# A four-batch attention and two mixture layers on one core: batch 0's queries and keys kept on chip, its v sums on VectorE, whole-word byte operations, and a new order for the ramp

## The chip, the core and the metric

One core of a Trainium2 chip runs the whole program. Its engines work from queues of their own, each strictly in order: TensorE (PE, with its weight loads as PEld), VectorE (DVE), ScalarE (ACT), GpSimd (POOL), and SyncE (SP), which here only starts transfers. POOL's queue can start transfers too, among them those that add what they bring to what already stands in SBUF. The metric is the device time of one execution in microseconds, and the median of several executions counts.

## The reference, cut to what matters

```python
# q, k, v: [4 batches, 8 heads, 576 rows, 64]
q_d, k_d, v_d = mean of q, k, v over groups of 4 rows          # 144 rows
out_d  = softmax(q_d @ k_d.T / 8) @ v_d                        # full attention, down-sampled
out_up = repeat(out_d, 4 times)
out_local = softmax(q @ k.T / 8, where |i - j| < 4) @ v        # a band of 7
x = (out_up + out_local) as [2304 tokens, 512]
# first layer, d_ff 2048
h = x @ w_in;  g = s * relu(h)**2 + b;  y = g @ w_out
# second layer, d_ff 1536
out = ((y @ w_a) * (y @ w_b)) @ w_out2
```

The weights arrive as 64-bit floats and are brought to a 32-bit format on chip. Each 32-bit matmul is made of three, from a high and a low part of either operand.

## The kernel before, in words

**Stages.** The first 768 tokens (the ramp: eight tiles of 96 rows, six of batch 0 and two of batch 1) get their attention at the start, while the weights of the first layer come in. `down(b, hp, ...)` is the down-sampled attention of one head pair `hp` of batch `b`, `tile_job` the local attention of a 96-row tile on TensorE. The later rows get their local attention on VectorE (`unit`), spread over the first layer's run. That layer works through six blocks of 384 tokens; in each, 16 iterations (`a_iter`) make a slice `h` of d_ff by 12 matmuls (L1030 to L1032), the square on ScalarE (L1047 to L1054), its low part `gl` on VectorE (L1058), and 12 matmuls that add to `acc` (L1073 to L1075). The second layer follows, from about 541 us on.

**Weights.** The first layer has 32 slices, two for an iteration (one of w_in, one of w_out). `w_words` unpacks the 64-bit words of a slice of 512 KB: `z_fn` (ScalarE, L334) scales the high word, `a_fn` (ScalarE, L345, called the byte operation here) turns some of the low bits of the high word into a number in the low word, `s_fn` (VectorE, L350) makes the sign, `b_fn` (VectorE, L358) puts the parts together. Then `h_fn` (ScalarE, L374) and `l_fn` (VectorE, L379) make the high and the low part. The finished slices stay in slots of the tag `w`, of which there are 33, for all six blocks, so this is done once. Before the change `a_fn` has four forms, by `k % 4`: it reads 16-bit halves or single bytes, and writes whole 32-bit words or 16-bit halves.

**The ramp.** For a head pair of batch 0, k and q are loaded (L271) into `dk` and `dq` and summed over groups of four rows on VectorE (L572, into `kd`, `qd`). v of a head pair comes in two loads `dv` and is summed by two additions on GpSimd (L595, L596, into `vp`). The scores go through TensorE (L610), the maximum (VectorE L624, L627), the exponentials (ScalarE L637), the normalisation (VectorE L645 to L652), transposes (TensorE L661, ScalarE L673), the product with `vp` (TensorE L681, `o`), and a copy into `up` (ScalarE L693). For each of the eight tiles q and k come again, as `tq` and `tk` (192 and 204 KB); scores at L760 over a mask (L754), maximum at L773, exponentials at L787, normalisation at L795 to L802, transposes at L810 and L820, product with `tv` at L828, and the sum with `up` at L842, which gives `x`; L493 and L497 split it. For batch 1 and later the sum of v over groups of four is made by transfers (`pool_in`): SP brings the first row of each group into `pv` (L539), and six transfers from POOL's queue (L541) add the three others, two chains of three.

**What sets the order.** No order is written out. Every piece of work is a task with an engine, an estimated duration, buffers that it takes and frees, and a due time. `Program.order` plans them all by a greedy rule: it takes the task that can start first, by due time among equals, and gives out the instructions in that order; each engine's queue is the result. Due times come from `target(idx)`, the planned time of an iteration, `T0` plus a number of `STEP`s, less the constants `DUE_*`; a planned result can be used `SEEN` later. The tables give the buffers of each tag, `MAX_STAGED` how many raw slices may be in SBUF. Before the change the planner has the adding transfers on an engine of their own, `GQ`, though they stand in POOL's queue.

## Time and profile before

| | |
|---|---|
| median of three runs | 978.01 us (977.96 to 978.42) |
| the profiled execution | 977.19 us |
| its span | 975.4 us |
| mean granted TensorE clock | 0.977 of full speed |
| busy: PE, DVE, ACT, POOL | 95%, 81%, 53%, 8% of the span |
| last weight slice of the first layer finished | 170.6 us from the span's start |
| first iteration of blocks 0 to 5 begins | 84.7, 171.3, 253.0, 327.9, 405.6, 474.1 us |
| the first layer's last iteration ends, about | 541 us |

Times in the trace are counted from the start of the span; the profiled execution takes 1.8 us more than its span, and stands 0.8 us below the median. In the views a group of instructions is named by line, engine and operation, with the tile it writes, an arrow, and the tiles it reads; what follows in brackets is the idle time of the engine just before it, and the work that ended that idle time. The granted clock is a share of 2.4 GHz. PE's busy time at half the clock counts double what the same work takes at the full one.

### The profile page before, as it was taken

To read this page: it belongs to the slowest core of one execution; us is meant where nothing else is said; L and a number is where in the kernel's file an instruction comes from. 1 tells how busy PE (TensorE), PEld (TensorE's weight loads), DVE (VectorE), ACT (ScalarE), POOL (GpSimd) and SP (SyncE) were. 2 spreads that over 40 slices of the span, in tenths; PEclk is the share of its full clock that TensorE was granted. 3 is DMA by queue.
4 is the path that set the end of the run, shared out by engine and by line. 5 is a ranking of instruction groups with operands and counts; after the bars stand their busy time and mean duration, and the time that the engine had idled before them with its cause. 6 is when DMAs were issued, how large, how long until landed. Compare 5 with 4: busy or idle time off the path is not lost.

```text
span 975.4 us, 14509 instructions
## 1 busy us (share of the span) xinstructions
PE 930.3 (95%) x5371; PEld 858.5 (88%) x5371; DVE 787.2 (81%) x1377; ACT 520.4 (53%) x1144; POOL 76.7 (8%) x86
## 2 busy tenths in 40 slices
PE   8589699999899999999999999999999999999997
PEld 4357699999799999999999999998999998999995
DVE  5378888899999999997776899978977779777753
...
GB/s 181 151 231 201 275 165 44 199 78 89 147 106 100 121 121 66 98 65 51 164 169 230 229 72 124 64 22 23 173 22 23 22 22 11 98 22 23 0 1 66
DMA packets 48159, 99.19 MB, mean 102 GB/s; under 512 B 6536, under 2 KB 22248, under 8 KB 47704
## 3 DMA queue, kind: packets, MB, share of 16 engines
...
q8 instruction: 42, 0.69, 0.3%
...
## 4 chain that ended last, share of the span: by engine, by line
PE 79%; DVE 9%; ACT 5%; DMA 3%; issue 2%; POOL 1%; SPq 0%; ACTq 0%; POOLq 0%
PE ab L1304 26%; PE h L1030 6%; PE h L1032 6%; PE acc L1073 6%; PE h L1031 6%; PE acc L1074 6%; PE acc L1075 6%; PE acc L1446 5%; PE acc L1445 5%; PE acc L1444 5%; DMA pv<-in_vd_dram 2%; ACT w L345 1%; DVE pr L940 1%; DVE xo L1181 1%; PE sc L610 1%
## 5 line engine op out<-in xcount | busy, mean ns | idle before, releaser
L1304 PE MATMUL ab<-xo,w 128*128 128x384 f32 x1370 | 276.9, 339 | 1.0 <-DVE w L1334 0.5
L1304 PEld LDWEIGHTS ab<-xo,w 128*128 128x128 f32 x1370 | 246.7, 189 | 16.9 <-DVE u L1378 0.8
L1030 PE MATMUL h<-xsh,w 128*128 128x384 f32 x384 | 132.8, 346 | 1.6 <-ACT u L1047 0.8
L1073 PE MATMUL acc<-gh,w 128*128 128x384 f32 (+1 forms) x384 | 132.5, 345 | 0.5 <-ACT w L345 0.5
L1074 PE MATMUL acc<-gl,w 128*128 128x384 f32 x384 | 130.3, 339 | 0.7 <-DVE gl L1058 0.7
L1032 PE MATMUL h<-xsh,w 128*128 128x384 f32 x384 | 130.4, 340 | 0.2 <-DVE w L379 0.2
L1031 PE MATMUL h<-xsl,w 128*128 128x384 f32 x384 | 130.4, 340 | 0.0
L1075 PE MATMUL acc<-gh,w 128*128 128x384 f32 (+1 forms) x384 | 129.9, 338 | 0.0
L1047 ACT ACTIVATE u<-h 128x384 f32<-128x384 f32 x96 | 48.1, 501 | 123.2 <-PE h L1032 118.3
L1420 ACT ACTIVATE gh<-u 128x384 fp32r<-128x384 f32 x68 | 35.8, 526 | 90.5 <-DVE u L1381 54.4
L1030 PEld LDWEIGHTS h<-xsh,w 128*128 128x128 f32 x384 | 73.3, 191 | 4.8 <-issue 2.3
L1073 PEld LDWEIGHTS acc<-gh,w 128*128 128x128 f32 x384 | 72.5, 189 | 2.6 <-issue 1.3
L1074 PEld LDWEIGHTS acc<-gl,w 128*128 128x128 f32 x384 | 72.6, 189 | 1.6 <-DVE gl L1058 1.6
L1032 PEld LDWEIGHTS h<-xsh,w 128*128 128x128 f32 x384 | 73.2, 191 | 0.6 <-DVE w L379 0.6
L1031 PEld LDWEIGHTS h<-xsl,w 128*128 128x128 f32 x384 | 73.3, 191 | 0.0
L1075 PEld LDWEIGHTS acc<-gh,w 128*128 128x128 f32 x384 | 72.5, 189 | 0.0
L1058 DVE TENSOR_TENSOR gl<-u,gh 128x384 fp32r<-128x384 f32 x96 | 54.0, 562 | 16.8 <-ACT gh L1054 16.5
L1328 ACT ACTIVATE w<-ab 128x384 f32<-128x384 f32 x32 | 15.7, 491 | 92.9 <-PE ab L1304 89.0
L345 ACT ACTIVATE w<-w 128x512 int32<-128x512 uint8 (+3 forms) x63 | 63.6, 1025 | 0.0
L350 DVE TENSOR_SCALAR w<-w 128x512 uint16<-128x512 f32 x63 | 47.5, 765 | 14.2 <-ACT w L345 14.0
L1054 ACT ACTIVATE gh<-u 128x384 fp32r<-128x384 f32 x96 | 50.6, 528 | 2.4 <-PE acc L1075 0.4
L1051 ACT ACTIVATE u<-u 128x384 f32<-128x384 f32 x96 | 50.7, 528 | 1.9
...
## 6 DMA issues: line engine op xcount, KB each, us to landing
...
```

The costliest lines, as they stand in the source:

```text
L345: A_.activation(out=halves()[:, :, 0] if k % 2 else low, in_=src, func=ACTF.Copy, scale=scale, bias=bias)
L1030: nc.tensor.matmul(out=st["h"], lhsT=w[:, 0, k], rhs=hi[:, k], start=(k == 0), stop=False)
L1031: nc.tensor.matmul(out=st["h"], lhsT=w[:, 0, k], rhs=lo[:, k], start=False, stop=False)
L1032: nc.tensor.matmul(out=st["h"], lhsT=w[:, 1, k], rhs=hi[:, k], start=False, stop=(k == HP - 1))
L1051: A_.activation(out=st["u"], in_=st["u"], func=ACTF.Square)
L1054: A_.activation(out=st["hi"][:, :n], in_=st["u"], func=ACTF.Copy)
L1058: V.tensor_tensor(out=st["lo"], in0=st["u"], in1=st["hi"][:, :n].bitcast(F32), op=ALU.subtract)
L1073: nc.tensor.matmul(out=acc, lhsT=wh, rhs=st["hi"], start=(f == 0), stop=False)
L1074: nc.tensor.matmul(out=acc[:, :n], lhsT=wh, rhs=st["lo"], start=False, stop=False)
L1075: nc.tensor.matmul(out=acc, lhsT=wl, rhs=st["hi"], start=False, stop=(f == FA - 1))
L1304: nc.tensor.matmul(out=o, lhsT=w[:, k], rhs=x, start=(not more and k + n == 0), stop=(k == 1 and n == 2), skip_group_check=more,)
L1444: nc.tensor.matmul(out=acc, lhsT=gh, rhs=w[:, 0], start=first, stop=False)
```

## The change

1. **q and k of batch 0 stay.** The loads of `down(0, hp, ...)` go into eight of the `w` slots (`wide_in`), with nothing to wait for, and stay there until all six tiles of batch 0 have their scores (`free_fn` then frees the slots). These tiles have no `tq` and `tk` loads any more; their score matmuls read a window of the kept k and q, 99 or 102 columns wide.
2. **v of batch 0 is summed on VectorE**, by one `tensor_reduce` of 72x512 into 72x128 for each of the eight halves, in place of two additions on GpSimd.
3. **The byte operation** has one form: it reads 16-bit halves and writes whole 32-bit words. Its planned duration goes from 0.9 to 0.56 us.
4. **The adding transfers** are planned on POOL, 1.25 us each, with a result that counts as landed 6.0 us later; `GQ` is gone.
5. **The ramp is planned anew**: `T0`, `STEP`, `LEAD`, the due times, `MAX_STAGED` (3 to 4), the buffers of `dq`, `dk`, `tq`, `tk`. Batch 1's down-sampled attention is due relative to `target(FA)`, the start of block 1, and no longer to `target(0)`, the start of block 0.

```diff
 DOWN_ENG = [("DVE", "DVE")] * 4
-MAX_STAGED = 3
+MAX_STAGED = 4
-T0, STEP = 36.0, 3.95 / 384
-LEAD = 20.0
-DUE_DOWN = (12.0, 2.5, 0.0, 8.0)
-DUE_TILE = (4.0, 5.0, 25.0)
-DUE_JOB = (14.0, 12.0, 15.0)
+T0, STEP = 40.2, 4.018 / 384
+LEAD = 26.6
+DUE_DOWN = (12.1, 7.8, 2.1, 22.5)
+DUE_NEXT = (60.0, 0.0)
+DUE_TILE = (8.3, 20.6, 22.0)
+DUE_JOB = (11.6, 11.7, 14.9)
...
         def a_fn(picks):
             low = st["low"] = words()[:, :, 0]
-            if k % 4 < 2:
-                src, scale, bias = halves()[:, :, 1], 2.0 ** -13, -4095.5 * 2.0 ** -13
-            else:
-                src = st["s"].rearrange("p a m -> p (a m)").bitcast(U8).rearrange("p (m c) -> p m c", c=8)[:, :, 3]
-                scale, bias = 2.0 ** -5, -15.5 * 2.0 ** -5
-            A_.activation(out=halves()[:, :, 0] if k % 2 else low, in_=src, func=ACTF.Copy, scale=scale, bias=bias)
-
-        add("ACT", 0.9, a_fn, [("st", k)], [("low", k)])
+
+            A_.activation(out=low, in_=halves()[:, :, 1], func=ACTF.Copy, scale=2.0 ** -13, bias=-4095.5 * 2.0 ** -13)
+
+        add("ACT", 0.56, a_fn, [("st", k)], [("low", k)])
...
+    def wide_in(p):
+        return slot(p[0], F32).rearrange("p a m -> p (a m)")[:, :S]
...
                 t[kh] = add(
-                    "GQ" if r else "SP", 1.3, fn, (), [("pv", b)] if r == 3 else (), () if r + kh else [("pv",)], (), due,
-                    [t[kh]] if r else [t[0]] if kh else after,
+                    "POOL" if r else "SP", 1.25, fn, (), [("pv", b)] if r == 3 else (), () if r + kh else [("pv",)], (), due,
+                    [t[kh]] if r else [t[0]] if kh else after, seen=6.0,
                 )
...
-            st["k"] = new(ph, "dk", [128, S])
+            st["k"] = whole["k", b, hp] = wide_in(p) if b == 0 else new(ph, "dk", [128, S])
...
-        load(l_q, 128 * HP * TQ * 4, writes=[("tq", i)], acq=[(names["tq"],)], after=after)
-        load(l_k, 128 * HP * TW * 4, writes=[("tk", i)], acq=[(names["tk"],)], after=after)
+        if b:
+            load(l_q, 128 * HP * TQ * 4, writes=[("tq", i)], acq=[(names["tq"],)], after=after)
+            load(l_k, 128 * HP * TW * 4, writes=[("tk", i)], acq=[(names["tk"],)], after=after)
+
+        k0, k1 = max(0, 3 - t0), min(TW, S + 3 - t0)
...
-                        out=sc[h][:, hp], lhsT=st["q"][h * D:h * D + D, hp], rhs=st["k"][h * D:h * D + D, hp],
+                        out=sc[h][:, hp, k0:k1], lhsT=qk("q", hp)[h * D:h * D + D], rhs=qk("k", hp)[h * D:h * D + D],
...
     for hp in range(HP):
-        down(0, hp, "r", DOWN_ENG[hp], "POOL", target(0) - DUE_DOWN[0] + DUE_DOWN[1] * hp)
+        down(0, hp, "r", DOWN_ENG[hp], "DVE", target(0) - DUE_DOWN[0] + DUE_DOWN[1] * hp)
...
-    pool_in(1, P.made["open", "r"], target(0))
+    pool_in(1, P.made["open", "r"], target(FA) - DUE_NEXT[0])
     for hp in range(HP):
-        down(1, hp, "r", ("POOL", "POOL"), "POOL", target(0))
+        down(1, hp, "r", ("POOL", "POOL"), "POOL", target(FA) - DUE_NEXT[0] + DUE_NEXT[1] * hp)
```

How the order of the queues changes shows at three places. On SP, the first transfers of the program; `dk`, `dq`, `tq`, `tk` are batch 0's k and q before. Before:

```order
L271 DMA dk<-in_kT_dram 128x576
L271 DMA dq<-in_qT_dram 128x576
L292 DMA tq<-in_bmask_dram 96x306
L271 DMA tq<-in_tq_dram 128x384
L271 DMA tk<-in_tk_dram 128x408
L271 DMA dk<-in_kT_dram 128x576
L271 DMA dq<-in_qT_dram 128x576
L271 DMA tq<-in_tq_dram 128x384
L271 DMA tk<-in_tk_dram 128x408
L287 DMA ident<-in_ident_dram 128x128
```

and after, where `w` is one of the kept slots:

```order
L272 DMA w<-in_kT_dram 128x576
L272 DMA w<-in_qT_dram 128x576
L272 DMA w<-in_kT_dram 128x576
L272 DMA w<-in_qT_dram 128x576
L272 DMA w<-in_kT_dram 128x576
L272 DMA w<-in_qT_dram 128x576
L272 DMA w<-in_kT_dram 128x576
L272 DMA w<-in_qT_dram 128x576
L293 DMA tq<-in_bmask_dram 96x306
L288 DMA ident<-in_ident_dram 128x128
```

All k and q of batch 0 now go out first; the mask and the identity matrix follow them. On POOL, from its first work on; `dv` and `vp` are batch 0's v sums, `pv` the adding transfers for batch 1. Before:

```order
L595 TENSOR_TENSOR dv<-dv 72x256
L596 TENSOR_TENSOR vp<-dv 72x128
L595 TENSOR_TENSOR dv<-dv 72x256
L596 TENSOR_TENSOR vp<-dv 72x128
L541 DMA pv<-in_vd_dram 72x4x128
L595 TENSOR_TENSOR dv<-dv 72x256
L596 TENSOR_TENSOR vp<-dv 72x128
L541 DMA pv<-in_vd_dram 72x4x128
L595 TENSOR_TENSOR dv<-dv 72x256
L596 TENSOR_TENSOR vp<-dv 72x128
L541 DMA pv<-in_vd_dram 72x4x128
```

and after, where L577 and L578 are batch 1's sums of k and q:

```order
L544 DMA pv<-in_vd_dram 72x4x128
L577 ISA
L577 TENSOR_TENSOR dk<-dk 128x144x2
L578 TENSOR_TENSOR kd<-dk 128x144
L577 TENSOR_TENSOR dq<-dq 128x144x2
L578 TENSOR_TENSOR qd<-dq 128x144
L544 DMA pv<-in_vd_dram 72x4x128 x4
L577 TENSOR_TENSOR dk<-dk 128x144x2
L578 TENSOR_TENSOR kd<-dk 128x144
L577 TENSOR_TENSOR dq<-dq 128x144x2
L578 TENSOR_TENSOR qd<-dq 128x144
L544 DMA pv<-in_vd_dram 72x4x128
```

Nothing of batch 0 stands in POOL's queue any more. On PE, around the first matmuls `h` of block 0; `o<-w,pv` belongs to batch 1's down-sampled attention, `pw` is a filler that reads zeros. Before:

```order
L760 MATMUL sc<-tk,tq 96x102 x8
L266 LDWEIGHTS wz
L266 MATMUL pw<-wz 128x408
L681 MATMUL o<-w,pv 64x144 x4
L1030 MATMUL h<-xsh,w 128x384
L1031 MATMUL h<-xsl,w 128x384
```

and after, where `o<-w,tv` is the product of a tile of batch 0:

```order
L850 MATMUL o<-w,tv 64x96 x8
L1052 MATMUL h<-xsh,w 128x384
L1053 MATMUL h<-xsl,w 128x384
L1054 MATMUL h<-xsh,w 128x384
L1052 MATMUL h<-xsh,w 128x384
L1053 MATMUL h<-xsl,w 128x384
L1054 MATMUL h<-xsh,w 128x384
L613 MATMUL sc<-kd,qd 72x144 x4
L664 MATMUL at<-ident,w 72x72 x8
L684 MATMUL o<-w,pv 64x144 x4
```

Before, all of batch 1's outputs stand ahead of the first `h`; after, half an iteration's `h` comes first, and batch 1's outputs lie among block 0's iterations.

## Rows read from the trace of the kernel before

**Rows 1.** Busy time by stretch: us, then PE, PEld, DVE, ACT, POOL; clock; DMA.

```profile
core 0: us, PE busy (x) PEld busy (x) DVE busy (x) ACT busy (x) POOL busy (x), PEclk, DMA share, GB/s
0.00:13.17 13.17, 8.97 (x43) 4.35 (x45) 4.30 (x11) 0.00 (x0) 0.20 (x4) 0.98 0.59 187
13.17:60.00 46.83, 32.29 (x273) 20.30 (x275) 23.08 (x54) 24.59 (x117) 22.15 (x30) 0.82 0.64 162
60.00:85.00 25.00, 24.15 (x247) 15.73 (x244) 23.15 (x54) 24.28 (x82) 6.67 (x8) 1.00 0.87 284
85.00:120.00 35.00, 26.02 (x170) 23.72 (x168) 28.46 (x58) 34.97 (x99) 4.87 (x3) 0.85 0.68 212
120.00:171.00 51.00, 50.40 (x309) 48.96 (x310) 42.35 (x79) 49.25 (x91) 3.59 (x3) 1.00 0.39 114
171.00:253.00 82.00, 76.88 (x457) 74.05 (x456) 77.07 (x106) 37.01 (x85) 13.51 (x13) 0.99 0.45 137
253.00:328.00 75.00, 74.85 (x438) 71.42 (x437) 69.49 (x92) 32.14 (x78) 15.19 (x14) 0.94 0.37 92
328.00:406.00 78.00, 78.00 (x496) 73.77 (x495) 75.89 (x134) 38.89 (x106) 10.57 (x11) 1.00 0.35 105
406.00:541.00 135.00, 134.96 (x775) 134.24 (x774) 103.80 (x152) 91.60 (x165) 0.00 (x0) 1.00 0.42 144
541.00:975.00 434.00, 423.76 (x2183) 391.99 (x2182) 339.61 (x647) 187.65 (x331) 0.00 (x0) 0.99 0.15 53
```

**Rows 2.** Last unpacking step of the last weight slice, timeline of DVE.

```profile
169.90 0.69 DVE L379 TENSOR_TENSOR w<-z,w 128x512 fp32r<-128x512 f32 x1 [0.15 <-ACT w L374]
```

**Rows 3.** ACT's first work, timeline of ACT, and the wait behind it, of DVE.

```profile
11.41 0.21 DVE L288 CAST identb<-ident 96x96 bf16<-96x96 f32 x1 [1.94 <-DMA ident<-in_ident_dram]
...
13.17 1.28 ACT L637 ACT_TABLE_LOAD   x1 [13.17 <-DVE nb L627]
```

**Rows 4.** ACT's waits, 13.2 to 60: total us, times, longest.

```profile
ACT up L693 <- PE o L681: 11.5, 3, 7.8
ACT w L820 <- DVE tnb L773: 3.6, 1, 3.6
```

**Rows 5.** PE's longest waits of that stretch, timeline of PE.

```profile
40.57 0.75 PE L681 MATMUL o<-w,vp 72*64 72x144 f32 x4 [7.68 <-POOL vp L596]
...
53.06 0.47 PE L681 MATMUL o<-e,vp 72*64 72x144 f32 x4 [4.06 <-POOL vp L596]
```

**Rows 6.** POOL between 28 and 41, its timeline; then the adding transfers' landing.

```profile
28.23 1.22 POOL L541 DMA_DIRECT2D pv<-in_vd_dram  x1 [4.80 <-DMA pv<-in_vd_dram]
...
38.02 1.21 POOL L541 DMA_DIRECT2D pv<-in_vd_dram  x1 [3.32 <-issue]
38.80 1.19 POOL L595 TENSOR_TENSOR dv<-dv 72x256 f32<-72x256 f32 x1
40.07 0.45 POOL L596 TENSOR_TENSOR vp<-dv 72x128 f32<-72x128 f32 x1
...
pv<-in_vd_dram POOLq DMA_DIRECT2D x6, 144.0 KB, 5.3
```

**Rows 7.** The byte operation to 170.5 by form: count, busy us, mean ns.

```profile
L345 ACT ACTIVATE w<-w 128x512 uint16<-128x512 uint8 x8 | 11.0, 1377 | 0.0
L345 ACT ACTIVATE w<-w 128x512 uint16<-128x512 uint16 x8 | 11.0, 1375 | 0.0
...
L345 ACT ACTIVATE w<-w 128x512 int32<-128x512 uint16 x8 | 5.7, 709 | 0.0
L345 ACT ACTIVATE w<-w 128x512 int32<-128x512 uint8 x8 | 5.7, 708 | 0.0
```

**Rows 8.** Two groups of DVE to 170.7, with idle time before them.

```profile
L773 DVE TENSOR_REDUCE tnb<-sc 96x4 f32<-96x408 f32 x16 | 8.5, 567 | 12.2 <-PE sc L760 12.2
...
L572 DVE TENSOR_REDUCE kd<-dk 128x144 f32<-128x576 f32 x4 | 3.0, 738 | 2.2 <-DMA dk<-in_kT_dram 2.2
```

**Rows 9.** Timeline of PE: block 0's first matmul, and two long waits.

```profile
84.68 0.44 PE L1030 MATMUL h<-xsh,w 128*128 128x384 f32 x1
...
104.75 1.92 PE L828 MATMUL o<-w,tv 102*64 102x96 f32 x16 [6.81 <-ACT w L820]
...
252.12 1.15 PE L661 MATMUL at<-ident,e 72*72 72x72 f32 x8 [2.20 <-DVE s L906]
```

More of the change, by code (lines that the diff above doesn't have):

```diff
@@ L11 @@
 I32 = mybir.dt.int32
-U8 = mybir.dt.uint8
 U16 = mybir.dt.uint16
@@ L115, in __init__, with add @@
         self.free = {k: [0.0] * n for k, n in free.items()}
-    def add(self, eng, dur, fn, reads=(), writes=(), acq=(), rel=(), due=1e9, after=(), lead=0.0, share=1.0):
+    def add(self, eng, dur, fn, reads=(), writes=(), acq=(), rel=(), due=1e9, after=(), lead=0.0, share=1.0, seen=None):
         t = Task()
+        t.seen = SEEN[eng] if seen is None else seen
         t.eng, t.dur, t.fn, t.acq, t.rel, t.due = eng, dur, fn, acq, rel, due
@@ L206, in order @@
                 a = a(t) if callable(a) else a
-                self.free[a].append(t.end + SEEN[t.eng])
+                self.free[a].append(t.end + t.seen)
             out.append((t, picks))
@@ L210, in order @@
                 u.left -= 1
-                u.ready = max(u.ready, t.end + (0.0 if u.eng == t.eng == "PE" else SEEN[t.eng]))
+                u.ready = max(u.ready, t.end + (0.0 if u.eng == t.eng == "PE" else t.seen))
                 if not u.left:
@@ L765, in tile_job, with free_fn @@
         ts = add(
-            "PE", 1.75, s_fn, [("tq", i), ("tk", i), "const"], [("tsc", i)], [wide, wide, E_SLOT[ph]],
-            [names["tq"], names["tk"]], after=[mm["dS", b, hp] for hp in range(HP)], lead=LEAD, share=0.55,
-        )
+            "PE", 1.75, s_fn, ([("tq", i), ("tk", i)] if b else [(x, (0, hp)) for x in ("dk", "dq") for hp in range(HP)]) + ["const"],
+            [("tsc", i)], [wide, wide, E_SLOT[ph]], [names["tq"], names["tk"]] if b else (),
+            after=[mm["dS", b, hp] for hp in range(HP)], lead=LEAD, share=0.55,
+        )
+        if b == 0:
+            mm.setdefault("whole", []).append(ts)
+            if len(mm["whole"]) == S // TQ:
+                def free_fn(p):
+                    pass
+                add("CTL", 0.0, free_fn, after=mm["whole"], rel=["w"] * 2 * HP)
         def m_fn(p):
```

24 lines of the change are left out of this document (15 added, 9 removed).

## The prediction

> **What bounds the kernel now.** Read the busy time by stretch first [rows 1]. From 171 us on PE is busy for 77 of 82 us, 75 of 75, 78 of 78 and 135 of 135, and in the second layer for 424 of 434: nothing that the change touches can take work from there. The first 171 us are another matter: PE is busy for 142 of them, much of that at a low clock or on fillers, so the start-up is set by something else. Between 60 and 171 it is ACT, with 24.3 of 25, 35.0 of 35 and 49.3 of 51 us. The stage ends when the last weight slice is unpacked, at 169.9 + 0.7 = 170.6 [rows 2]; block 0's last iterations take the slices as they come, and block 1 begins right behind. So the length of the ramp is an account of ACT: it starts at 13.2 [rows 3], works 24.6 + 24.3 + 35.0 + 49.3 = 133.1 us up to 171, and is idle for the rest, 157.8 - 133.1 = 24.7 us. Of these, 46.83 - 24.59 = 22.2 lie between 13 and 60.
>
> Where they come from: ACT waits there 11.5 us for the outputs `o` of the down-sampled attention and 3.6 for a tile's maximum [rows 4]. PE, in order, waits for `vp` of POOL just before: 7.7 us up to 40.6 and 4.1 up to 53.1 [rows 5]. POOL has the sums late because the adding transfers of batch 1 stand ahead of them in its queue, and the next may be issued only when the one before has landed: the waits of 4.8 and 3.3 us in front of such an issue, the sums right behind at 38.8 and 40.1 [rows 6]. DVE's 12.2 us for the tile scores [rows 8] is the same hold-up, one engine on, and ACT's 3.6 us too. So 11.5 + 3.6 = 15.1 us of ACT's idle time are due to v's sums; 22.2 - 15.1 = 7.1 are the ordinary hand-overs of the softmax chains.
>
> **The change part by part.**
>
> *The byte operation.* Of the 32 in the ramp, 16 write half words, at 1.375 us, and 16 whole words, at 0.709 [rows 7]. All become whole words: 16 x (1.376 - 0.709) = 10.7 us less ACT work. It lies on the engine that sets the stage's end, so it counts in full as long as ACT remains the bound. After the first layer the same operation runs 31 times more, but ACT is idle for more than half of that time [rows 1]: nothing.
> The Trainium skill ("ScalarE: Activation LUTs", section "What ACT_TABLE_LOAD costs") says that an ACTIVATE runs at one element a cycle a lane for fp32 and bf16 alike; 186 ns + 0.833 x 512 = 612 ns is its figure, with no word of the width written. By that this part would save nothing and the time would come out 10.7 us later than I forecast. The rows at 709 ns agree roughly, those at 1375 do not: writing half words is measured at twice the time, and the measurement decides.
>
> *v's sums on DVE.* POOL loses 16 additions, DVE gets eight reductions. No such one is in the trace; the nearest, of 576 elements a lane on 128 lanes, takes 738 ns [rows 8]; by elements 512/576 x 738 = 656 ns. Below, 0.45 us (POOL's own second addition of 128, [rows 6]), above, POOL's pair 1.19 + 0.45 = 1.64. I take 0.65, 8 x 0.65 = 5.2 us of DVE work (bounds 3.6 and 13.1). It falls into a stretch in which DVE is busy for 23.1 of 46.8 us. So it is covered; if it were not, it costs 5.2. What goes is POOL's place in the chain, the 15.1 us of ACT. Behind the sums the next thing late is the softmax hand-over, 7.1 us, which I leave as it is.
>
> *k and q kept.* Twelve loads go, 6 x (192 + 204) KB = 2.4 MB. No slot is waited for. But ACT's start hangs on the identity matrix, whose cast ended a 1.9-us wait at 11.4 [rows 3]; ahead of it, it included, stood 4 x 0.295 + 2 x 0.406 + 0.118 + 0.066 = 2.2 MB, and now 8 x 0.295 + 0.118 + 0.066 = 2.5 MB. 0.35 MB more at 187 GB/s [rows 1] is 1.9 us, so the cast comes at 13.3. Of the 1.8 us that lay between the cast and ACT's start, the two maxima now stand ahead of the cast; two short operations of 0.2 us and the hand-overs remain. I take a start of 14.0, 0.8 later (bounds 0 and 1.9). The narrower score windows are 99 for 102 columns at the two ends: nothing.
>
> *Bytes.* By rows 1, 2.5 + 7.6 + 7.1 + 7.4 + 5.8 = 30 MB were moved in 171 us; with 2.4 less in 145 us that is 193 GB/s, where 284 was reached between 60 and 85. Transfers do not bind.
>
> *Adding transfers and batch 1.* Six issues of 1.2 us, landing 5.3 us after issue [rows 6]. They now stand behind batch 1's own sums, and their results are read by PE after the first `h`. Four stand in a row: at 5.3 each, two chains side by side, some 11 to 21 us. If they come late, `o<-w,pv` blocks PE's queue, `h` behind it included; that is a rival below. POOL is free otherwise, so I count nothing.
> The Trainium skill ("SBUF — State Buffer", section "Who interferes with whom") says that a VectorE instruction with two SBUF inputs contends with a GpSimd instruction that reads SBUF, and that tensor_reduce on trn2 never does. By it the reductions would not disturb POOL. POOL's first addition took 1.19 us for its 256 elements, the second 0.45 for 128 [rows 6], which neither supports nor refutes it; the sum is the same by either.
>
> *The plan.* Block 0's first `h`, at 84.7 [rows 9], comes when four tiles are ready. The v stall and the loads of batch 1's chain no longer lie ahead of it; I walk the new order and put it at about 56 (50 to 65). It doesn't set the end: PE needs for block 0 and what lies among it 26.0 + 50.4 = 76.4 us by rows 1 in 85 to 171, less some 2 for the low clock; 56 + 74 = 130. The wait of 6.8 us at 98 to 104.7 [rows 9] lies in slack too. DVE has 4.3 + 23.1 + 23.2 + 28.5 + 42.4 = 121.5 us, with the sums 126.7; if it began 4.3 us before 13.2 and never waited, it ended at 135.6.
>
> **The sum.** ACT starts at 14.0, works 133.1 - 10.7 = 122.4, and waits 7.1 in the first part plus the 24.7 - 22.2 = 2.5 of the rest: 146.0, for 171 before: 25.0 gained. From there to the end of the first layer took 541 - 170.6 = 370 us and PE was busy for 365 of it: this length is kept by PE's and DVE's work (DVE 77 of 82, 69 of 75, 76 of 78), which the change leaves as it is. Its bounds: the stalls before 253, of which the 2.2 us for a unit's softmax is one [rows 9], with the low clock behind them (0.94 of 75, 4.5 us), could vanish: -9; or a unit, whose place in DVE's order shifts by some 5 to 9 us of work against the blocks, arrives late: +9. I take +1. The second layer: 0, bounds -3 and +3. The profiled execution's 977.2 - 25.0 + 1 = 953.2; the median stood 0.8 higher, which I leave in the range. **Forecast 953.0 us**.
>
> **The rivals.**
>
> *ACT and DVE lock each other.* With both engines at 122 and 127 us of some 132 to 137, each slice's five hand-overs between them may not pack. For: a slice goes ACT, DVE, ACT, DVE, and DVE has only some 10 us to spare (146 less 135.6). Against: between 60 and 85 both were busy for 24.3 and 23.2 of 25 us [rows 1], that is they packed. If ACT's idle time remained what it was (24.7), the gain would be the byte operation less the later start, 9.9: 967. Half-way, 960.
>
> *The byte operation saves nothing.* By the equal speed whatever is written the sum ends 10.7 us later, at 963.9; 16 rows at 1.375 us against 16 at 0.709 [rows 7] speak against it. The rule of the Trainium skill's page above is this one.
>
> *More than that.* The unit stalls and the low clock around 253 vanish, or the early hand-overs shrink since no tile waits for a load: up to 9 and 4 less: 940 to 946.
>
> *Adding transfers late.* The last lands after some 75 instead of 56; PE stands 19 us in block 0, of which 146 - 130 = 16 is its slack: 956; with half the clock behind that stall (10 us cost 5 more), up to 968.
>
> *PE at half clock through block 0: slower than before.* After the long wait at 98 to 104.7 the clock fell: 0.85 over 85 to 120 [rows 1]. With the iterations begun early and thinned out by batch 1's chain and by slices that come one by one, PE waits in every iteration, and the clock may not come back. Block 0's 74 us at full clock would then be 148, from 56 to 204, and block 1 would start 33 us later than now: some 1010. It decides against the kernel before from 82 us at half the clock on (82/2 + 33 = 74 in the 115 us between 56 and 171). Against: between 120 and 171, with the same slices arriving one by one, PE was busy for 50.4 of 51 us at clock 1.00 [rows 1].
>
> *It doesn't do what it says.* The score matmuls wait for all eight loads, or for the `w` slots; the v sums come late in DVE's own queue, as they stand behind softmax steps. Then PE waits as before, and about 977 less the byte operation, if ACT still binds: 966 to 977.
>
> **How the numbers follow.** Forecast (946 to 961) 0.50; lock or half of it (961 to 969) 0.18; better (938 to 946) 0.14; late adds beyond the forecast 0.04; the byte operation for nothing 0.01; not as it says 0.05, of which 0.04 within 0.2% of before; slower 0.06; 0.02 for something below 938. The range leaves out the slower case, the equal one and the ends: 940 to 968. A measurement of this kernel can tell about 0.2%, 2 us; faster by more: 0.90, within: 0.04, slower: 0.06.
>
> **What would show it.** Right: the last slice unpacked at about 146, all byte operations near 0.7 us, ACT idle for some 10 us from its start to there, no wait of PE for `vp` above 2 us, and 370 us from there to the first layer's end. The first `h` between 50 and 65. Wrong: ACT idle for 20 us again, with DVE busy before each wait (the lock); `o<-w,pv` with a wait of over 10 us (late adds); a granted clock near 0.5 over 60 to 140; a first layer that takes over 375 us behind the ramp, with waits for a unit's `s` or `o` at the block starts, by which the gain would be given back.

## The result and the profile after

| | before | after |
|---|---|---|
| median | 978.05 us (977.96 to 978.42, four runs) | 940.84 us (936.27 to 941.98, four runs) |
| profiled execution, its span | 977.19, 975.4 us | 939.76, 937.6 us |
| mean granted TensorE clock | 0.977 | 0.993 |
| last weight slice finished | 170.6 us | 142.0 us |
| from there to the end of the span | 804.8 us | 795.6 us |

The ratio is 0.961 (95% interval 0.9576 to 0.9644), a gain of 3.9%. Of 978.05 that is 939.9, just under the low end of the range, 940; the forecast was 953.0. Executions of one kernel differ by several us (5.7 among these four of the changed kernel; 7.0 over all those of the kernel before in the experiments, 972.85 to 979.85), so a difference of 1 or 2 us between two medians or two traces says little.

The whole difference of the spans, 37.8 us, lies in two places: the ramp ends 28.6 us earlier, and what follows it is 9.2 us shorter (8.4 of it in the first layer, 362.0 us for 370.4). First the stretches of the changed kernel, cut at its own events (ACT's start, the first h, the ramp's end, the starts of blocks 2, 3 and 4, the end of the first layer); columns as in [rows 1].

```profile
0.00:11.78 11.78, 10.62 (x53) 5.11 (x53) 4.51 (x12) 0.00 (x1) 0.20 (x4) 1.00 0.80 251
11.78:57.36 45.58, 38.07 (x414) 25.25 (x414) 43.81 (x97) 40.25 (x184) 19.23 (x21) 1.00 0.77 197
57.36:85.00 27.64, 24.15 (x174) 20.19 (x173) 25.39 (x54) 27.43 (x85) 3.97 (x4) 0.88 0.87 277
85.00:142.00 57.00, 55.41 (x334) 52.92 (x334) 51.54 (x97) 54.51 (x116) 5.55 (x4) 1.00 0.53 147
142.00:217.00 75.00, 74.81 (x443) 73.12 (x441) 69.57 (x92) 33.95 (x73) 11.96 (x9) 1.00 0.40 119
217.00:290.40 73.40, 73.40 (x461) 70.20 (x458) 71.16 (x97) 34.56 (x90) 19.40 (x18) 1.00 0.47 120
290.40:367.80 77.40, 77.17 (x487) 72.46 (x487) 74.45 (x132) 37.19 (x103) 8.90 (x11) 1.00 0.34 100
367.80:504.00 136.20, 136.20 (x785) 136.09 (x785) 112.40 (x166) 88.40 (x171) 0.00 (x0) 1.00 0.46 155
504.00:937.60 433.60, 423.61 (x2182) 391.77 (x2180) 337.51 (x643) 182.25 (x329) 0.00 (x0) 0.99 0.15 51
```

Before, ACT was idle for nearly half of 13 to 60 [rows 1]; now it is busy for 40.3 of 45.6 us before the first h and 27.4 of 27.6 and 54.5 of 57.0 behind it. The clock is 1.00 nearly everywhere; 57 to 85, with 0.88, is the exception. Between 142 and 217, which answers to 171 to 253 before, PE has hardly a gap any more, and the stage is 75 us long where it took 82. The second layer's 433.6 us are the 434 of before.

Single events, in the timelines of DVE, ACT and PE:

```profile
11.15 0.32 DVE L294 CAST bmaskb<-tq 96x306 bf16<-96x306 f32 x1 [1.14 <-DMA tq<-in_bmask_dram]
11.41 0.21 DVE L289 CAST identb<-ident 96x96 bf16<-96x96 f32 x1
11.78 1.28 ACT L640 ACT_TABLE_LOAD   x1 [11.78 <-DVE nb L630]
...
57.36 0.44 PE L1052 MATMUL h<-xsh,w 128*128 128x384 f32 x1
...
141.27 0.69 DVE L376 TENSOR_TENSOR w<-z,w 128x512 fp32r<-128x512 f32 x1
```

Two groups of ACT and DVE up to 150 (count, busy us, mean ns, idle time before):

```profile
L342 ACT ACTIVATE w<-w 128x512 int32<-128x512 uint16 x32 | 21.4, 678 | 0.0
L596 DVE TENSOR_REDUCE vp<-dv 72x128 f32<-72x512 f32 x8 | 8.2, 1032 | 0.0
```

The identity is cast at 11.4, as before [rows 3], though 0.35 MB more lie ahead of it: the first 11.8 us moved 251 GB/s, where the first 13.2 us before moved 187. Before, SP's queue stood there for 6.4 us at VectorE's work on the tiles loaded first (3.2 us for `nb`, 3.0 for `kd`, 0.2 for `qd`); now it doesn't wait for VectorE there. ACT starts 1.4 us earlier. All 32 byte operations take the short form.

### The profile page after: what moved, and what is told of

Read it like the earlier page. It is cut to its first block, busy times and chain, and to the rows that moved or that the text cites. A ratio compares the mean times of both kernels' runs of the same rounds, so it can differ in the third digit from the quotient of the medians.

```text
span 937.6 us, 14356 instructions
## 1 busy us (share of the span) xinstructions
PE 913.4 (97%) x5319; PEld 847.1 (90%) x5319; DVE 790.3 (84%) x1385; ACT 498.5 (53%) x1144; POOL 69.2 (7%) x70
## 4 chain that ended last, share of the span: by engine, by line
PE 81%; DVE 8%; ACT 4%; issue 3%; DMA 2%; POOL 1%; SPq 0%; ACTq 0%; POOLq 0%
PE ab L1326 27%; PE acc L1095 6%; PE acc L1096 6%; PE acc L1097 6%; PE h L1052 6%; PE h L1053 6%; PE h L1054 6%; PE acc L1468 5%; PE acc L1467 5%; PE acc L1466 5%; DVE pr L962 1%; DMA pv<-in_vd_dram 1%; DVE xo L1203 1%; DMA tq<-in_bmask_dram 1%; ACT w L342 1%
## 5 line engine op out<-in xcount | busy, mean ns | idle before, releaser
L1326 PE MATMUL ab<-xo,w 128*128 128x384 f32 x1232 | 264.5, 339 | 0.8 <-DVE w L1356 0.5
L1326 PEld LDWEIGHTS ab<-xo,w 128*128 128x128 f32 x1232 | 222.8, 189 | 15.3 <-DVE u L1400 1.0
L1052 PE MATMUL h<-xsh,w 128*128 128x384 f32 x384 | 131.0, 341 | 0.0
L1054 PE MATMUL h<-xsh,w 128*128 128x384 f32 x384 | 128.9, 336 | 0.0
L1442 ACT ACTIVATE gh<-u 128x384 fp32r<-128x384 f32 x68 | 35.7, 525 | 93.4 <-DVE u L1403 58.4
L1326 PE MATMUL ab<-xo,wx 128*128 128x384 f32 x280 | 77.5, 339 | 0.4 <-DVE u L1369 0.4
L1052 PEld LDWEIGHTS h<-xsh,w 128*128 128x128 f32 x384 | 72.1, 188 | 2.4 <-issue 2.0
L1054 PEld LDWEIGHTS h<-xsh,w 128*128 128x128 f32 x384 | 72.1, 188 | 0.0
L1468 PE MATMUL acc<-w,gl 128*128 128x512 f32 x159 | 62.6, 394 | 0.0
L1467 PE MATMUL acc<-w,gh 128*128 128x512 f32 x159 | 62.6, 393 | 0.0
L1466 PE MATMUL acc<-w,gh 128*128 128x512 f32 x159 | 62.4, 393 | 0.0
```

What stands on the lines that cost most here:

```text
L1052: nc.tensor.matmul(out=st["h"], lhsT=w[:, 0, k], rhs=hi[:, k], start=(k == 0), stop=False)
L1054: nc.tensor.matmul(out=st["h"], lhsT=w[:, 1, k], rhs=hi[:, k], start=False, stop=(k == HP - 1))
L1326: nc.tensor.matmul(out=o, lhsT=w[:, k], rhs=x, start=(not more and k + n == 0), stop=(k == 1 and n == 2), skip_group_check=more,)
L1466: nc.tensor.matmul(out=acc, lhsT=gh, rhs=w[:, 0], start=first, stop=False)
L1467: nc.tensor.matmul(out=acc, lhsT=gh, rhs=w[:, 1], start=False, stop=False)
L1468: nc.tensor.matmul(out=acc, lhsT=gl, rhs=w[:, 0], start=False, stop=last)
```

## Two accounts for the ramp

Each experiment below is read by the same account as in the prediction: ACT's start, plus its busy time up to the end of the last weight slice, plus its idle time. PE's busy time and clock in that stretch stand beside it, because the account turned out to need them. "Rest" is the span's end less the ramp's end. The median is that of all executions, the other columns are read from one trace.

| kernel | median us | ramp's end | ACT start + busy + idle | PE busy, clock | first h | rest |
|---|---|---|---|---|---|---|
| before | 976.6 to 978.1 | 170.6 | 13.2 + 132.7 + 24.7 | 132.4, 0.92 | 84.7 | 804.8 |
| b_byte | 975.47 | 168.0 | 13.3 + 124.1 + 30.6 | 130.4, 0.92 | 83.7 | 803.2 |
| b_next | 968.04 | 172.0 | 13.7 + 132.3 + 26.0 | 134.5, 0.84 | 69.6 | 796.3 |
| b_next_byte | 964.29 | 165.8 | 14.0 + 123.6 + 28.2 | 131.6, 0.87 | 66.4 | 796.4 |
| b_sums1st | 982.32 | 178.9 | 11.6 + 130.8 + 36.5 | 134.9, 0.87 | 91.3 | 801.7 |
| b_vdve | 969.22 | 168.8 | 13.1 + 131.8 + 23.9 | 135.3, 0.85 | 78.6 | 798.7 |
| b_vdve_next | 969.08 | 171.2 | 13.5 + 132.2 + 25.5 | 136.5, 0.84 | 69.3 | 796.3 |
| b_vdve_next_byte | 958.94 | 157.6 | 13.3 + 121.4 + 22.9 | 125.6, 0.91 | 68.6 | 799.5 |
| b_due | 974.98 | 171.6 | 13.1 + 132.5 + 26.1 | 135.2, 0.89 | 85.8 | 802.7 |
| after | 940.84 | 142.0 | 11.8 + 122.2 + 8.0 | 117.6, 0.97 | 57.4 | 795.6 |
| a_oldbyte | 953.66 | 154.2 | 11.1 + 131.5 + 11.6 | 124.8, 0.93 | 61.9 | 797.7 |
| a_tiles | 953.92 | 153.7 | 12.9 + 122.7 + 18.1 | 125.8, 0.93 | 60.4 | 796.3 |
| a_vpool | 945.61 | 146.0 | 11.4 + 122.0 + 12.6 | 117.6, 0.96 | 63.1 | 795.2 |
| a_next0 | 942.95 | 144.1 | 10.7 + 122.4 + 11.0 | 120.3, 0.96 | 67.2 | 797.0 |
| a_due | 950.25 | 144.2 | 11.4 + 122.3 + 10.5 | 120.8, 0.95 | 60.3 | 802.4 |
| a_bytes | 960.41 | 156.5 | 11.9 + 123.6 + 21.0 | 131.7, 0.92 | 79.5 | 805.0 |
| a_lo4 | 962.24 | 156.2 | 11.9 + 123.1 + 21.2 | 126.4, 0.91 | 63.8 | 804.7 |

## Experiments: the rest of the first layer

Two kernels move only the due times of later rows.

```diff
# a_due: the changed kernel with
-DUE_DOWN = (12.1, 7.8, 2.1, 22.5)
+DUE_DOWN = (12.1, 7.8, 0.0, 8.0)
-DUE_JOB = (11.6, 11.7, 14.9)
+DUE_JOB = (14.0, 12.0, 15.0)
# b_due: the kernel before with
-DUE_DOWN = (12.0, 2.5, 0.0, 8.0)
+DUE_DOWN = (12.0, 2.5, 2.1, 22.5)
-DUE_JOB = (14.0, 12.0, 15.0)
+DUE_JOB = (11.6, 11.7, 14.9)
```

> The changed kernel with the due times of later rows (those of the units, and of batch 2's head pairs) as they were before; the ramp's plan is untouched. In the changed kernel the stretch from the ramp's end to the first layer's end is 9 us shorter than before, because DVE's order has one score pass of the fourth unit (2 to 4 us) and one softmax of batch 2 (2.7 us) less ahead of the third unit's x. Theory (it is these due times): block 2 starts some 7 us later again with PE waiting ahead of it and a low clock behind it, 948 to 950 us. Rival (the earlier ramp alone removes that wait): 941 us.

> The kernel before with the changed due times of later rows alone; the ramp's plan is untouched. Theory: the ramp ends at 170.6 as before, block 2 starts some 4 to 8 us earlier than 253.0, and the time is 969 to 974 us. Rival (those due times matter only with the new ramp): 978 us.

a_due took 950.25 us (ratio to before 0.9729, 0.971 to 0.9749; the changed kernel has 0.961). The mechanism shows in DVE's order ahead of block 2. Block 2 needs the third unit's `x` (through its high part `xsh` and its low part `xsl`), and on PE's queue the `at` of a softmax `e` of batch 2 stands ahead of it. In the kernel before, timeline of DVE, `x` and `e` both come behind two score passes (L879 and L885, 4 us each) of the fourth unit:

```profile
240.71 2.02 DVE L879 TENSOR_TENSOR pr<-bq,bk 128x1792 f32<-128x1792 f32 x1
...
243.39 2.01 DVE L885 TENSOR_REDUCE s<-pr 128x28 f32<-128x1792 f32 x1
...
245.78 2.02 DVE L879 TENSOR_TENSOR pr<-bq,bk 128x1792 f32<-128x1792 f32 x1
...
248.26 2.00 DVE L885 TENSOR_REDUCE s<-pr 128x28 f32<-128x1792 f32 x1
...
250.54 0.65 DVE L986 TENSOR_TENSOR x<-bt,up 128x512 f32<-128x512 f32 x1
...
251.23 0.74 DVE L652 TENSOR_TENSOR e<-e,sm 72x576 f32<-72x576 f32 x1
```

In the changed kernel `x` comes at 213.2, ahead of both passes and right behind one softmax step, and `xsl` ends at 216.4:

```profile
213.15 0.68 DVE L1008 TENSOR_TENSOR x<-bt,up 128x512 f32<-128x512 f32 x1
213.75 2.01 DVE L901 TENSOR_TENSOR pr<-bq,bk 128x1792 f32<-128x1792 f32 x1
215.68 0.68 DVE L494 TENSOR_TENSOR xsl<-x,xsh 128x512 fp32r<-128x512 f32 x1
216.28 2.01 DVE L907 TENSOR_REDUCE s<-pr 128x28 f32<-128x1792 f32 x1
```

and in a_due the fourth unit's two score passes (now L901 and L907) and most of a second softmax of batch 2 stand ahead of it again, in a queue that has no idle time in these 12 us:

```profile
213.82 2.03 DVE L901 TENSOR_TENSOR pr<-bq,bk 128x1792 f32<-128x1792 f32 x1
215.76 0.81 DVE L627 TENSOR_REDUCE nb<-sc 72x2 f32<-72x288 f32 x2
216.50 2.00 DVE L907 TENSOR_REDUCE s<-pr 128x28 f32<-128x1792 f32 x1
...
218.89 2.01 DVE L901 TENSOR_TENSOR pr<-bq,bk 128x1792 f32<-128x1792 f32 x1
...
221.37 2.00 DVE L907 TENSOR_REDUCE s<-pr 128x28 f32<-128x1792 f32 x1
...
223.65 0.65 DVE L1008 TENSOR_TENSOR x<-bt,up 128x512 f32<-128x512 f32 x1
224.34 0.74 DVE L655 TENSOR_TENSOR e<-e,sm 72x576 f32<-72x576 f32 x1
225.14 0.68 DVE L494 TENSOR_TENSOR xsl<-x,xsh 128x512 fp32r<-128x512 f32 x1
```

PE then stands twice in a_due, and in the kernel before at the same two places for 1.16 and 2.20 us (the second is in [rows 9]); timeline of PE:

```profile
222.37 0.66 PE L992 MATMUL bt<-ident,o 128*128 128x128 f32 x4 [1.15 <-ACT e L640]
225.23 0.67 PE L664 MATMUL at<-ident,e 72*72 72x72 f32 x8 [2.21 <-DVE s L928]
225.70 0.42 PE L1052 MATMUL h<-xsh,w 128*128 128x384 f32 x1
```

The view names `s` for the second wait, but what this `at` reads is `e`, ready at 225.1; `xsh` is ready at 225.0 and `xsl` at 225.8. So two paths, both behind the score passes, end together there. Block 2 starts 81.5 us behind the ramp's end instead of 75.1, the clock drops to half for 6.8 us behind the wait, and the rest is 802.4 us long instead of 795.6. The theory holds (948 to 950 us expected): 6.8 of the 9.2 us come back with the old due times. b_due took 974.98 (0.9984, 0.9971 to 0.9996), between its theory (969 to 974) and its rival (978): one score pass stands ahead of `x` in place of two, but one more product (L879) ahead of `xsl`; PE waits 2.3 us for the `gl` of an iteration of block 1 instead, block 2 starts at 251.1, and the rest is 802.7.

So the due times work only through the order that the planner makes of them. Counted on DVE from the ramp's end to that `xsl`, the kernel before, b_byte, a_due, a_bytes and a_lo4 have eight score passes and two softmaxes of batch 2, and a rest of 802.4 to 805.0, though a_bytes and a_lo4 have the new due times. Of the others, b_due apart, all eleven have six or seven finished passes and one softmax there, and a rest of 795.2 to 801.7, six of them with the old due times.

## Experiments: the byte operation, and batch 1's place

```diff
# b_byte: the kernel before with the new a_fn; a_oldbyte: the changed kernel with the old one
+            A_.activation(out=low, in_=halves()[:, :, 1], func=ACTF.Copy, scale=2.0 ** -13, bias=-4095.5 * 2.0 ** -13)
```

> The kernel before with the one whole-word form of the byte operation and nothing else; its planned duration stays at 0.9 us, so every queue keeps its order. Theory (ACT binds the ramp): the ramp's end comes 10.7 us earlier, at 160, all else as before: 967.3 us. Rival (ACT and DVE hold each other up): the saved ACT time turns into ACT idle time, half of it or more: 972 or above. Rival (equal speed whatever is written): 978.

> The changed kernel with the four old forms of the byte operation back, planned at 0.56 us, so every queue keeps its order. Theory: ACT is still the bound, the ramp ends 10.7 us later, at 152.7, and the kernel takes 951.5 us. Rival: the changed ramp has DVE as its bound, so the loss is under 6 us: below 947.

a_oldbyte: 953.66 us (0.9771, 0.9744 to 0.9797), its ramp 12.2 us longer: ACT's busy time rises by 9.3 us and its idle time by 3.6. The theory holds for the changed kernel. b_byte: 975.47 (0.9985, 0.9975 to 0.9994), the ramp only 2.6 us shorter: ACT works 8.6 us less and waits 5.9 more. The theory fell for the kernel before. The first rival has the time right (972 or above) but the partner only in part: ACT now waits more for PE than for DVE. Its waits for `h`, from 60 to the ramp's end, in b_byte and then in the kernel before (total us, times, longest):

```profile
ACT u L1043 <- PE h L1028: 5.1, 9, 0.8
...
ACT u L1047 <- PE h L1032: 1.1, 3, 0.6
```

Its waits for DVE rose from 0.8 to 3.6 us there. PE's rows of b_byte, by stretch, show why:

```profile
85.00:120.00 35.00, 26.70 (x185) 24.56 (x185) 29.04 (x58) 33.43 (x101) 3.89 (x3) 0.85 0.68 207
120.00:168.00 48.00, 48.00 (x293) 47.16 (x290) 39.76 (x75) 42.01 (x84) 3.59 (x3) 1.00 0.39 115
```

From 120 to the ramp's end PE has not a gap. In the kernel before it is 50.4 of 51 us [rows 1], which I had read only as cover for ACT: with a first h at 84.7 the work of block 0 itself takes PE to 168. So two accounts ended together there, ACT's and PE's. If PE's late start is the second one, an earlier first h alone must also gain nothing at the ramp's end, and both edits together more than their sum:

```diff
# b_next: the kernel before with batch 1 due as in the changed kernel
-    pool_in(1, P.made["open", "r"], target(0))
+    pool_in(1, P.made["open", "r"], target(FA) - 60.0)
-        down(1, hp, "r", ("POOL", "POOL"), "POOL", target(0))
+        down(1, hp, "r", ("POOL", "POOL"), "POOL", target(FA) - 60.0)
# b_next_byte: both edits
```

> The kernel before with batch 1 due 60 us ahead of block 1 instead of at the start of block 0, and nothing else; GpSimd still has three adding transfers among the v sums. Theory (v's sums behind the transfers are the hold-up of the ramp): the waits for vp stay, and the time is within 6 us of 978. Rival (batch 1 ahead of the first h on PE is the hold-up): the first h comes at 65 to 75 and the time is 955 to 968 us.

> The kernel before with two edits that were each tried alone: batch 1 due 60 us ahead of block 1, and whole-word byte operations (every queue as with the first edit alone). Alone, the byte operation moved the ramp's end from 170.6 to 168.0, and the due time moved it to 172.0 though the first h came 15 us earlier. Theory (ACT's account and PE's account, first h plus block 0's work, both ended at 171, so either edit alone only meets the other): together the ramp ends at 159 to 163 and the time is 955 to 960 us. Rival (the two gains add up): ramp's end at 169, 965 to 968 us.

b_next: 968.04 us (0.99, 0.9881 to 0.9919), at the upper end of the rival's range. Its first h comes at 69.6, 15.1 us earlier, as the rival said, but its ramp ends at 172.0, and PE still waits 7.0 us for `vp`, as the theory said; the 9 us of gain lie in the rest, by the order of the third unit's `x`. b_next_byte: 964.29 (0.9876, 0.9859 to 0.9892), ramp's end 165.8. So -2.6 and +1.4 alone, -4.8 together: more than the sum, but short of the theory's 159 to 163, and the time is just under the rival's 965 to 968. What keeps the early start from paying is in good part the clock; b_next by stretch:

```profile
60.00:120.00 60.00, 46.73 (x341) 36.99 (x340) 48.59 (x98) 54.46 (x161) 13.51 (x13) 0.76 0.73 227
120.00:172.00 52.00, 52.00 (x318) 51.17 (x315) 42.46 (x80) 48.63 (x91) 1.19 (x1) 0.99 0.36 110
```

PE is idle for 13.3 us of 60 to 120, has a clock of 0.76 there (1.2 GHz for (1 - 0.76) x 2 x 60 = 29 us), and then runs without a gap at 2.4 GHz to the end. From the first h to the ramp's end it takes 102.4 us for the 85.9 of before: 2.6 of these 16.5 us are idle time, and it has 26.6 us at 1.2 GHz for 10.3. A row of 128x384 matmuls goes at one per 0.32 us at that clock and one per 0.175 at the full one (a_due, 229 and 220 us), 1.8 times and not quite the double, so the low clock costs some 7 us; what is left, some 7, is mostly work that used to stand ahead of the first h, three of batch 1's four outputs among it. The low clock is the prediction's slow-clock rival, on a smaller scale and in another kernel. The changed kernel has 6.8 us at 1.2 GHz between its first h and the ramp's end (0.88 over 57 to 85).

The same due time undone in the changed kernel:

```diff
# a_next0: the changed kernel with
-    pool_in(1, P.made["open", "r"], target(FA) - DUE_NEXT[0])
+    pool_in(1, P.made["open", "r"], target(0))
-        down(1, hp, "r", ("POOL", "POOL"), "POOL", target(FA) - DUE_NEXT[0] + DUE_NEXT[1] * hp)
+        down(1, hp, "r", ("POOL", "POOL"), "POOL", target(0))
```

> The changed kernel with batch 1's down-sampled attention and its adding transfers due at the start of block 0, as before; the planner then puts all of batch 1's outputs ahead of the first h on PE. Theory (batch 1 ahead of the first h holds up block 0, and PE has too little slack to make it good): the first h comes 10 us or more after 57, and the time is 948 to 960 us. Rival (ACT binds the ramp, and the same ACT work in another order ends as early): 938 to 945 us.

942.95 us (0.9643, 0.9624 to 0.9662): the rival. Batch 1's scores and two of its four outputs stand ahead of the first h, which comes 10 us later, and the ramp ends only 2.1 later, with the clock at 1.00 from there on. Here PE had slack and ACT had not, as the prediction's account has it.

## Experiments: who sums v, and what stands ahead

```diff
# b_sums1st: the kernel before, adding transfers behind the v sums
-    pool_in(1, P.made["open", "r"], target(0))
+    pool_in(1, [t for hp in range(HP) for kh in range(2) for t in P.made["vp", (0, hp), kh]], target(0))
# b_vdve: the kernel before, v summed on VectorE; b_vdve_next, b_vdve_next_byte: with the edits above
-        down(0, hp, "r", DOWN_ENG[hp], "POOL", target(0) - DUE_DOWN[0] + DUE_DOWN[1] * hp)
+        down(0, hp, "r", DOWN_ENG[hp], "DVE", target(0) - DUE_DOWN[0] + DUE_DOWN[1] * hp)
# a_vpool: the changed kernel with
-        down(0, hp, "r", DOWN_ENG[hp], "DVE", target(0) - DUE_DOWN[0] + DUE_DOWN[1] * hp)
+        down(0, hp, "r", DOWN_ENG[hp], "POOL", target(0) - DUE_DOWN[0] + DUE_DOWN[1] * hp)
```

> The kernel before with one edit: the adding transfers of batch 1 are planned only behind all of batch 0's v sums, which stay on GpSimd; POOL's queue then has the sums first. Theory (the transfers ahead of the sums held up the ramp): PE's waits of 7.7 and 4.1 us for vp are gone, the first h comes 10 to 15 us before 84.7, the ramp ends at 156 to 160, and the time is 956 to 965 us. Rival (batch 1's outputs stand ahead of the first h on PE, so the late transfers now block there): the first h stays near 85 and the time near 978.

> The kernel before with v of batch 0 summed by VectorE as in the changed kernel, and nothing else. Theory: as with the transfers moved, PE no longer waits for vp; the ramp ends at 156 to 160, the time is 956 to 965 us. Rival (the sums' 8 us of VectorE work come into the ramp's path): 5 us or more above the kernel that only moves the transfers.

> The kernel before with v's sums on VectorE and batch 1 due 60 us ahead of block 1, the byte operation as before. Against the kernel that has the new byte operation besides (958.9 us). Theory (with the hold-ups gone ACT binds, and the byte operation is worth its 10 us): 967 to 971 us. Rival (other stalls bind there): 959 to 963 us.

> The kernel before with three of the changes: v's sums on VectorE, batch 1 due 60 us ahead of block 1, whole-word byte operations. Tile loads, adding transfers and all other constants are as before. Theory (these take both hold-ups and the ACT work away, and PE begins block 0 early, so the byte operation counts): 948 to 958 us, some 12 to 17 above the changed kernel, which has the kept q and k and the later rows' due times besides. Rival (the byte operation still gives 1 us, as in the kernel before): 965 us or more.

> The changed kernel with v of batch 0 summed on GpSimd again; the planner now puts these sums ahead of most adding transfers by itself. Theory (the engine of the sums doesn't matter, only what stands ahead of them): 937 to 945 us, vp not waited for by more than 2 us. Rival (GpSimd's two additions are too slow, or the transfers get ahead again): 950 us or more, with PE waiting for vp.

b_sums1st is slower than before by half a per cent: 982.32 us (1.0046, 1.0022 to 1.007), so its theory fell and the rival came. PE does not wait for `vp` any more; timeline of its waits over 3 us:

```profile
60.63 1.24 PE L610 MATMUL sc<-kd,qd 64*72 64x144 f32 x8 [9.08 <-POOL qd L575]
72.38 0.71 PE L610 MATMUL sc<-kd,qd 64*72 64x144 f32 x8 [3.51 <-POOL qd L575]
77.98 0.75 PE L681 MATMUL o<-w,pv 72*64 72x144 f32 x4 [4.21 <-DMA pv<-in_vd_dram]
```

GpSimd now comes to batch 1's own sums and transfers later, and PE meets them before its first h: 16.8 us of waits in place of 11.7. b_vdve has none of the v sums on GpSimd and is 969.22 (0.9922, 0.9892 to 0.9951), with a ramp only 1.8 us shorter, which neither its theory (956 to 965) nor its rival foresaw; most of its gain lies in the rest. It too has a new wait, of PE for batch 1's `qd`:

```profile
47.49 1.24 PE L610 MATMUL sc<-kd,qd 64*72 64x144 f32 x8 [6.79 <-POOL qd L575]
```

b_vdve_next is 969.08 (0.992, 0.9892 to 0.9947), as its theory had it, ramp's end 171.2; with the byte operation besides, 958.94 (0.9815, 0.9791 to 0.9838), ramp's end 157.6, 1 us above its theory. These 13.6 us of ramp are not the byte operation's alone: b_vdve_next_byte has its planned duration of 0.56 us too, and the planner puts DVE's and ACT's queues in another order. Where every queue keeps its order, the byte operation is worth 2.6 us in the kernel before, 6.2 with b_next and 12.2 in the changed kernel. a_vpool is 945.61 (0.9686, 0.9648 to 0.9724), between its theory and its rival: 4 us more of ramp, and again not by `vp` but by a wait of 5.3 us for `qd` of batch 1. So the engine of v's sums is worth 2 to 4 us of ramp, whichever end one starts from. Between 13 and 60 ACT did wait 15.1 us behind those sums, but when they are gone the next in the queue is late.

## Experiments: q and k kept, and GpSimd for part of the weights

```diff
# a_tiles: the changed kernel without the kept q and k: loads into dk and dq, tq and tk for every tile
-            st["k"] = whole["k", b, hp] = wide_in(p) if b == 0 else new(ph, "dk", [128, S])
+            st["k"] = new(ph, "dk", [128, S])
-RAMP_BUFS = {"dq": 2, "dk": 2, "dv": 2, "qd": 1, "kd": 1, "vp": 4, "tq": 1, "tk": 1, "tv": 2, "e": 1, "x": 1, "z": 2}
+RAMP_BUFS = {"dq": 1, "dk": 1, "dv": 2, "qd": 1, "kd": 1, "vp": 4, "tq": 2, "tk": 2, "tv": 2, "e": 1, "x": 1, "z": 2}
...
# a_bytes: the changed kernel, tiles of batch 0 loaded as well, and waited for
-        if b:
+        if True:
             load(l_q, 128 * HP * TQ * 4, writes=[("tq", i)], acq=[(names["tq"],)], after=after)
# a_lo4: the changed kernel with
-W_ENG_A = ["DVE"]
+W_ENG_A = ["DVE", "DVE", "DVE", "POOL"]
```

> The changed kernel with q and k loaded again for each of batch 0's tiles, as before (2.4 MB more, and slots to wait for). Theory (transfers don't bind the ramp): 938 to 946 us, first h at 57 to 61. Rival (the loads hold up the tiles or the weights): the first h at 65 or later and 950 us or more.

> The changed kernel with q and k kept, but the tiles' twelve loads of q and k issued as well (2.4 MB more, and the scores wait for them; the matmuls read the kept ones). The kernel that truly loads them again took 953.9 us, 13 more than the changed one. Theory (what it lost lies in the bytes and in the scores' wait for each tile's load): 948 us or more. Rival (it lost by the few slots for k and q of the head pairs, which make the sums and softmaxes wait for each other): 939 to 945 us.

> The changed kernel with the low part of every fourth weight slice made on GpSimd in place of VectorE: 8 x 0.7 = 5.6 us off VectorE, which was busy for 120 of 130 us of the ramp, on an engine that is mostly idle. Theory (ACT alone binds the ramp): within 2 us of the changed kernel, 938 to 943. Rival (VectorE binds as much as ACT): 3 to 5 us faster, 934 to 938. A loss of over 3 us would mean that GpSimd's slower subtraction holds up the iterations that want these slices.

a_tiles: 953.92 us (0.9764, 0.9736 to 0.9792). The rival in time, though not by a late first h: 11.7 us more of ramp, 10.1 of it ACT's idle time. The first h comes at 60.4, but the tiles' `x` come 7 to 10 us later than in the changed kernel (the fourth tile's low part ends at 61.1 against 54.1, the sixth's at 69.5 against 59.7). By stretch:

```profile
12.95:60.40 47.45, 40.74 (x414) 26.59 (x410) 39.83 (x87) 36.69 (x169) 12.30 (x14) 0.96 0.81 216
60.40:85.00 24.60, 19.98 (x159) 15.86 (x157) 18.51 (x41) 18.25 (x57) 8.29 (x8) 0.72 0.60 188
```

ACT is idle for 10.8 us before the first h and for 6.4 of 60 to 85, where transfers are busy for 0.60 only, as against 0.87 in the changed kernel. So it is not the rate of the transfers that binds there. SP's queue stands at waits for 42 of the first 70 us, but so it does in the changed kernel (48), so their sum is not the cause either. a_bytes: 960.41 (0.9825, 0.9796 to 0.9854), as its theory had it: its ramp ends at 156.5, and its first h is at 79.5, behind batch 1's scores and three of its outputs. Its tiles' scores come 10 us apart (33.9, 45.9, 56.0), which would fit one slot for `tq` and `tk`, but is not shown to be the cause. Its rest is 805.0, by the order of the units again. Both kernels pay 12 to 14 us of ramp for the loads; whether by the bytes, by the places of the waits in SP's queue or by a plan whose constants were set for kept q and k, these two don't tell apart. That stays open.

Two of these kernels close the sum of the ramp. b_vdve_next_byte and a_tiles differ by the new plan alone (its constants, the adding transfers planned on POOL), and a_tiles and the changed kernel by the kept q and k with their buffers. So the ramp's end goes from 170.6 to 157.6 with the v sums, batch 1's due time and the byte operation, to 153.7 with the new plan, and to 142.0 with q and k kept: 13.0, 3.9 and 11.7 us in this order. The constants of the plan were not tried one by one.

a_lo4: 962.24 (0.9841, 0.9807 to 0.9874), neither theory nor rival, but the loss named last. GpSimd needs 1.45 us for a low part that DVE makes in 0.70. The group of GpSimd up to 160:

```profile
L376 POOL TENSOR_TENSOR w<-z,w 128x512 fp32r<-128x512 f32 x8 | 11.6, 1450 | 54.9 <-ACT w L371 45.5 <-DVE w L347 9.4
```

and ACT's longest wait in the iterations, timeline of ACT:

```profile
109.56 0.66 ACT L335 ACTIVATE z<-w 128x512 f32<-128x512 f32 x1 [4.81 <-POOL w L376]
```

The 1.45 us explain little of this wait. The high part of that slice was ready at 102.6 at the latest (L371); timeline of POOL:

```profile
107.03 1.20 POOL L544 DMA_DIRECT2D pv<-in_vd_dram  x1 [4.96 <-issue]
107.77 1.75 POOL L376 TENSOR_TENSOR w<-z,w 128x512 fp32r<-128x512 f32 x1
```

The low part stood behind an adding transfer of batch 1, for whose issue POOL's queue waited 5.0 us, and the slice's buffer `z`, which ACT writes next, was held until it was done: the same hold-up that batch 0's v sums had before. The plan differs elsewhere too (first h 6.4 us later, the longer order ahead of block 2). So ACT's idle time goes from 8.0 to 21.2 us, and whether DVE binds as much as ACT stays untested. None of the kernels tried is faster than the changed one.

## Why the prediction was right or wrong

**The direction and the outline of the ramp** were right, its end nearly: 142.0 measured, 146.0 forecast, a gain of 28.6 us for 25.0 (counted from 171, where the last slice is done at 170.6). Term by term: ACT's start 11.8 for 14.0 (the rate of 187 GB/s was read in a stretch in which loads waited for slots; without these it was 251); its busy time 122.2 for 122.4; its idle time 8.0 for 9.6. But two terms behind the idle time were mis-sized against each other. The v sums were put at 15.1 us; taken alone in either kernel they move the ramp by 1.8 and 4.0. The kept q and k were put at nothing ("transfers do not bind"); without them the ramp is 11.7 us longer. I had shown that the bytes fit under the rate, and not asked what else the loads, their slots and their places in SP's queue may hold up; which of these it is stays open. That the sum came so close is luck: both errors lie in the same 15 us, with opposite signs.

**The byte operation** was sized right in the kernel in which it counts: 10.7 forecast, 12.2 of ramp measured. The Trainium skill's rate ("ScalarE: Activation LUTs", section "What ACT_TABLE_LOAD costs") gives 186 ns + 0.833 ns an element, by which an estimate for every form is 612 ns. Here 32 whole-word operations took 678 ns each, against 1375 for the half-word forms [rows 7], and a_oldbyte's ACT is busy for 9.3 us more. For the half-word forms the measurement decides against it.

**ACT as the one bound of the kernel before** was wrong. b_byte and b_next show a second account that ended at the same time: PE's, from its first h at 84.7 through block 0, from 120 on without a gap. The rows for it were shown (PE busy for 50.4 of 51 us), and the prediction used them only for PE's need in the changed kernel. It did little harm to the sum, because the change moves both.

**v's sums on DVE**: 8 x 1.03 = 8.2 us for the 5.2 taken, inside its bounds of 3.6 and 13.1. DVE is busy for 120.7 of 130.2 us; ACT's waits for it in that stretch are 4.6 of the 8.0.

**After the ramp** lies the main error, the step that failed: +1 taken, -9.2 measured, just past the bound of -9. The prediction held that this length "is kept by PE's and DVE's work"; from the ramp's end to the first layer's end it took 362.0 us, not 370. It said that a unit's place in DVE's order shifts by 5 to 9 us of work against the blocks, and took the shift for a risk without saying in which direction. The order shows it: ahead of the third unit's `x`, on which block 2's start hangs, DVE has two score passes and one softmax of batch 2 less. The 2.2 us of [rows 9], which the prediction put down to a unit's softmax, were the wait for batch 2's `e` behind the same passes. a_due measures the step at 6.8 us of rest. Of the remaining 2.4 us the traces show one part: behind that wait the clock was at 1.2 GHz for 10.2 us before and for 6.8 in a_due, a difference of 1.5 us of work; now it is not at all.

**The rivals.** "More than that" came true, by the first of its two reasons: the stalls and the low clock around 253 are gone. The lock of ACT and DVE did not come: both were busy for over 120 of 130 us. The late adding transfers did not come in the changed kernel (PE has no wait for `pv` in its ramp); in b_sums1st they did, with 4.2 us for `pv`, and made it slower than before. The clock at half did not come in the changed kernel but for 6.8 us; in b_next it ate about half of the early start, and b_next_byte has as much of it (27.9 us at 1.2 GHz behind the first h).

**The range** ended at 940 because the better case was given 938 to 946 at 0.14. With the direction of the shift read from the order, the forecast would have been 953.2 - 1 - 9 = 943.
